# Random-feature attention and a gated MLP in one program: the high part of the gated product is cast by VectorE instead of ScalarE, and the transpose of z moves into a step's MLP share

## The chip, the cores and the metric

The program runs on one core of one Trainium2 chip. Its time is the device time of one execution in microseconds; three executions of the kernel before took 1170.35, 1173.78 and 1174.83 us, median 1173.78 us. The engines are named as in the profile: PE (TensorE matmuls; PEld its weight loads), DVE (VectorE), ACT (ScalarE), POOL (GpSimd), SP (SyncE, which here only issues transfers). Each engine works through its own queue in order and waits on semaphores of the others.

## The reference, cut to what matters

```python
batch, n_heads, seq, head_dim = (8, 8, 576, 64); n_features = 128
n_tokens, d_model, d_ff = (4608, 512, 1536)

def phi(x):                                   # random features
    proj = np.einsum('bhsd,md->bhsm', x, omega)
    h = proj - np.sum(x * x, axis=-1, keepdims=True) / 2.0
    h = h - np.max(h, axis=-1, keepdims=True)
    return np.exp(h) / np.sqrt(m)
q_p, k_p = (phi(q_s), phi(k_s))
kv = np.einsum('bhsm,bhsd->bhmd', k_p, v)
z = np.sum(k_p, axis=2)
num = np.einsum('bhsm,bhmd->bhsd', q_p, kv)
den = np.einsum('bhsm,bhm->bhs', q_p, z)[..., None] + 1e-06
x = (num / den) as [4608, 512]                # attention output = MLP input
g = x @ w_gate;  silu = g * (1.0 / (1.0 + np.exp(-g)));  val = x @ w_val
out = (silu * val) @ w_out
```

All arrays are float32. The MLP is computed with every float32 factor split into a high part (rounded to the PE's faster `fp32r` form) and a low part (the remainder), three matmuls per product: high times high, high times low, low times high.

## The kernel before

**Two halves.** Until about 570 us the program runs the attention in 76 steps, and beside it the MLP for the first three token tiles of 512 (visits 0 to 11: three tiles times four sets of three slices of 128 of the hidden width). After that the six remaining tiles are taken in pairs, with seven products in place of eight per 2x2 block (lines 989 to 1151). The step loop is at lines 1125 to 1150: a step takes one group of 256 rows of q and one of k through transposes (`pt`, L411), projections (`pp`, L434), row maxima and sums on DVE (L448 to L458), exponentials on ACT (`ph`, L470), the accumulation of k's features with v (`kvacc`, L572), and, for q, transposes of the features (`ptq`, L596, copied to `qt`, L598) and the output product (`xt`, L646 or L653).

**What sets the order.** From step `EARLY` on, the tuple `GROUPED` names a step's parts. Between them stand six entries `SHARE`; at each one `give` draws matmuls from the generator `stream` (the MLP) until the MLP is as far as a precomputed course says. The framework's scheduler then fixes each engine's queue when the program is built, beginning from the order of the code; engines do not reorder at run time.

**z.** For batches 4 to 7 (`b >= BPOOL`) the denominators are made by POOL and DVE from rows of z (`q_den`, L528 to L538), so z, the 65th column of the accumulator, must become a row. When a half batch's accumulation ends, `kv_finalize` copies the accumulator out of PSUM on ACT (`kvr`, L486); PE transposes the four z columns (`zp`, L492) in the one PSUM buffer of `ps_att`, ACT copies them (`zs`, L494), SP writes them to DRAM (L496) and `load_z` reads them back broadcast to all partitions (L508). This happens eight times.

**The gated product.** In `stream`, each of the 12 visits has three slices f. For each, PE makes `v` (12 matmuls, L689), DVE multiplies it out of PSUM with the silu of the gate (`sl`, L785), ACT casts the product to its high part (`hh`, L788), POOL subtracts to get the low part (`hl`, L789). The products wait until the next visit's gates are done, when `down` multiplies them with `w_out` (`o`, L698) and DVE adds the result to `acc` (L728). PE's three PSUM buffers `ps_m` hold `g`, `v` and `o` in turn; they come free when ACT has made `sl` from `g` (L765), DVE has read `v` (L785) and DVE has read `o` (L728).

**The handover.** When the last attention transfer has landed, its memory goes to the second half: `first_x` (L844 to L861) loads and splits the next two tiles, and `seven_steps` (L895 to L915) makes the first sums of weights, mostly on DVE, while PE finishes visits 10 and 11. The weights of the first half are converted by a chain over ACT, DVE and POOL (L277 to L295, until about 490 us) and reloaded from DRAM by SP (`wraw`, L334), split by ACT (L251) and POOL (L252).

Of the kernel before, what the change touches and what calls it, by code (L numbers as in the profile page):

```python
# [23 lines left out]
def kernel(  # L24
# [11 lines left out]
    nc = tc.nc  # L36
# [61 lines left out]
    def ps_att(name, shape):  # L98
        return ps_a.tile(shape, F32, name=name, tag="b")
# [30 lines left out]
    def slots(n, kind):  # L130

        if not 0 <= n < NS:
            return []
        return [(i, b, g, (kgroups if kd == "k" else qgroups)[g]) for i, (kd, b, g) in enumerate(steps[n]) if kd == kind]
# [25 lines left out]
    def mm1_us(w):  # L160
        return 3 * NC * (w / 2.4 + 13) * US
# [321 lines left out]
    def kv_finalize(b, a2):  # L483
        acc = kvacc.pop((b, a2))
        raw = att.tile([P, 4, VW], F32, name=f"kvr{b}_{a2}", tag="kvr", bufs=4)
        nc.scalar.copy(raw, acc)  # L486
        for j in range(2):
            kvst[b, 2 * a2 + j] = raw[:, 2 * j : 2 * j + 2, :]
        if b >= BPOOL:

            zp = ps_att(f"zp{b}_{a2}", [4, P])
            nc.tensor.transpose(zp, raw[:, :, D], ident)  # L492
            zs = att.tile([4, P], F32, name=f"zs{b}_{a2}", tag="zs")
            nc.scalar.copy(zs, zp)  # L494
            zd = dram.tile([4, P], F32, name=f"zd{b}_{a2}", tag="zd", bufs=4)
            nc.sync.dma_start(zd, zs)  # L496
            zds[b, a2] = zd

    zds = {}
    zbc = {}  # L500

    def load_z(n):
# [38 lines left out]
    def q_norm(n):  # L541
        n -= NLAG
        for _, b, g, gr in slots(n, "q"):
            if b < BPOOL:
                continue
            dn = dns.pop((b, g))
            phv = box["q", b, g].rearrange("p c (h m) -> p (c h) m", m=M)
            nc.gpsimd.tensor_tensor(
                phv, phv,
                dn[:, 2].rearrange("p c (h o) -> p (c h) o", o=1).broadcast_to([P, 2 * CH, M]),  # L550
                op=ALU.mult,
            )
# [147 lines left out]
    def avail(j):  # L700
        return sum(TILES[j]) <= cols_done[0]
# [4 lines left out]
    def fetch_x(j):  # L706

        xt[j] = [xres.tile([P, NPAIR, T], F32R, name=f"x{e}{j}", tag=f"x{e}") for e in "hl"]
        for c in range(NC):
            raw = moe.tile([P, T], F32, name=f"xraw{j}_{c}", tag="wraw", bufs=3)  # L710
            nc.sync.dma_start(raw, x_dram[j][:, c, :])
            hi, lo = (t[:, c] for t in xt[j])
            nc.scalar.copy(hi, raw)
            nc.gpsimd.tensor_tensor(lo, raw, hi.bitcast(F32), op=ALU.subtract)

    def down(j, k_, ht, wts, next_set, tt):
        fs = sorted(ht)
        po = ps_moe(f"o{j}_{k_}_{tt}", [P, DM])
        for n, f in enumerate(fs):
            need(f, 2)  # L720
            land((f, 2))
            mm2(po, ht[f], weights[f, 2] if wts is None else wts[f], tt, n == 0, n == len(fs) - 1)
        if k_ == 0:
            acc[j, tt] = accp.tile([P, DM], F32, name=f"acc{j}_{tt}", tag="acc")
            nc.scalar.copy(acc[j, tt], po)
        else:
            a_ = acc[j, tt]
            nc.vector.tensor_tensor(a_, po, a_, op=ALU.add)  # L728
        if k_ == (NPF if j in paired else NSET) - 1:
            a_ = acc.pop((j, tt))  # L730
            for o in range(0, P, RES):
                nc.sync.dma_start(rows_of(TILES[j][0] + tt * P + o), a_[o : o + RES, :])
        if next_set is not None and tt == TILES[j][1] // P - 1:
            for f in next_set:
                load_weights(f, 2)

    def stream():

        todo = []
        for vi, (j, s_, k_) in enumerate(visits):  # L740
            nxt = visits[vi + 1] if vi + 1 < len(visits) else None
            new_set = nxt and nxt[1] != s_
            final = nxt is None
            w = TILES[j][1]
            while not avail(j):
                if todo:
                    down(*todo.pop(0))
                    yield MM2
                else:
                    yield None  # L750
            if j not in xt:
                fetch_x(j)
            xs = [t[:, :, 0:w] for t in xt[j]]
            fs = range(s_ * FA, (s_ + 1) * FA)
            pg, ht = {}, {}
            for f in fs:
                need(f, 0)
                land((f, 0))
                pg[f] = ps_moe(f"g{vi}_{f}", [P, T])[:, 0:w]
                mm1(pg[f], weights[f, 0], xs)  # L760
                yield mm1_us(w)

            for f in fs:
                sl = moe.tile([P, T], F32, name=f"sl{vi}_{f}", tag="sl", bufs=FA)[:, 0:w]
                nc.scalar.activation(sl, pg[f], AF.Silu)  # L765
                pg[f] = sl
            if new_set:
                for f in fs:
                    load_weights(nxt[1] * FA + f - fs[0], 0)
            if final:  # L770
                make_seven((0, 0), 0, fetch((0, 1), 0))
            while todo:
                down(*todo.pop(0))
                yield MM2

            if nxt and nxt[0] not in xt and avail(nxt[0]) and last_visit[nxt[0] - NXB] < vi:
                fetch_x(nxt[0])
            for f in fs:
                need(f, 1)
                land((f, 1))  # L780
                pv = ps_moe(f"v{vi}_{f}", [P, T])[:, 0:w]
                mm1(pv, weights[f, 1], xs)
                yield mm1_us(w)
                h = pg[f]
                nc.vector.tensor_tensor(h, pv, h, op=ALU.mult)  # L785
                hh = moe.tile([P, T], F32R, name=f"hh{vi}_{f}", tag="hh", bufs=FA)[:, 0:w]
                hl = moe.tile([P, T], F32R, name=f"hl{vi}_{f}", tag="hl", bufs=FA)[:, 0:w]
                nc.scalar.copy(hh, h)  # L788
                nc.gpsimd.tensor_tensor(hl, h, hh.bitcast(F32), op=ALU.subtract)  # L789
                ht[f] = hh, hl  # L790
                if new_set:
                    load_weights(nxt[1] * FA + f - fs[0], 1)
            if final:
                make_seven((0, 0), 1, fetch((0, 1), 1))
            for f in fs if vi else ():
                land((f, 2))
            wts = {f: weights[f, 2] for f in fs} if vi else None
            then = range(nxt[1] * FA, nxt[1] * FA + FA) if new_set else None
            todo = [(j, k_, ht, wts, then, tt) for tt in range(w // P)]
        yield from pair_rounds(todo)  # L800
# [266 lines left out]
    def give(us):  # L1067
# [40 lines left out]
        SHARE,  # L1108
        SHARE,
        SHARE,  # L1110
        lambda n: q_norm(n + 1),
        q_mult,
        SHARE,
# [72 lines left out]
```

## Time and profile before

| | |
|---|---|
| three executions | 1170.35, 1173.78, 1174.83 us (median 1173.78) |
| the profiled execution | 1174.65 us, of which 1172.6 us from its first to its last instruction |
| granted TensorE clock, mean | 0.998 |
| busy shares of the span | PE 98%, DVE 60%, ACT 58%, POOL 50% |
| steps with MLP work beside them | about 120 to 570 us |
| pairs of tiles | about 620 us to the end |

A row of a group view reads: source line, engine, operation, output and inputs by name, shapes, count; then busy time in us and the mean of one in ns; then the idle time of that engine just before these instructions and what ended it. A row of the timeline reads: start in us, duration in us, engine, line, operation; in brackets how long the engine had been idle and who released it. PE's matmuls overlap, so their durations are not their spacing: a 128x512 matmul is listed with 0.39 us and follows its predecessor after about 0.23 us.

### The profile page before, as it was taken

Reading aid. Unit: us, or ns where it says so; the run is one execution under the profiler, and the core shown is the slowest. Engines: PE = TensorE matmul, PEld = TensorE weight load, DVE = VectorE, ACT = ScalarE, POOL = GpSimd, SP = SyncE. Lnnn points to the kernel's source line nnn. Section 1 sums busy time; section 2 is a strip of 40 time slices with the busy share of each in tenths; the row PEclk is TensorE's granted clock in tenths of the full one; section 3 lists DMA queues with packets and bytes.
Section 4 is the critical chain, followed back from the end, with each engine's and each line's share of the span. In section 5 each row is a group of like instructions: output and inputs, shape, how many; then the busy total and the mean of one; then the engine's idle time right before and its main releaser. Section 6 shows DMA issues by size and latency. Waiting matters only on the chain.

```text
span 1172.6 us, 18833 instructions
## 1 busy us (share of the span) xinstructions
PE 1145.0 (98%) x6633; PEld 948.3 (81%) x6633; DVE 703.3 (60%) x1266; ACT 684.7 (58%) x1541; POOL 588.6 (50%) x515
## 2 busy tenths in 40 slices
PE   8999999999999999999999999999999999999998
PEld 7888778888787778767778788888878888888886
DVE  3777576454666665556373566666566666456654
ACT  4888887877766866857434544444444445444441
POOL 3332353253656775586335655544455543555551
PEclk9999999999999999999999999999999999999999
DMA  6655355654445543431445111124211111211103
GB/s 141 160 135 132 102 161 142 185 151 122 129 130 139 143 140 102 109 86 55 135 109 151 57 55 55 54 65 124 63 50 46 52 52 46 81 55 54 46 18 72
DMA packets 173965, 114.30 MB, mean 97 GB/s; under 512 B 125840, under 2 KB 144304, under 8 KB 173872
## 3 DMA queue, kind: packets, MB, share of 16 engines
q1 hardware_dynamic: 172528, 112.78, 35.1%
q8 instruction: 52, 0.85, 0.3%
q10 hardware_dynamic: 1344, 0.33, 0.1%
q14 instruction: 41, 0.34, 0.1%
HBM read 87.88 MB, written 25.18 MB: 96 GB/s over the span
## 4 chain that ended last, share of the span: by engine, by line
PE 80%; DVE 7%; ACT 4%; POOL 3%; DMA 3%; issue 2%; SPq 0%; POOLq 0%; DVEq 0%; ACTq 0%
PE o L698 22%; PE a L928 16%; PE c L928 8%; PE g L689 6%; PE pp L434 6%; PE kvacc L572 5%; PE v L689 4%; PE d L928 4%; PE pt L411 3%; PE po L613 3%; PE ptq L596 2%; ACT ph L470 2%; PE xt L653 1%; POOL wlo L252 1%; PE xt L646 1%
## 5 line engine op out<-in xcount | busy, mean ns | idle before, releaser
L470 ACT ACTIVATE ph<-pp,st 128x128 f32<-128x128 f32 x576 | 157.3, 387 | 12.8 <-DVE st L458 12.3
L728 DVE TENSOR_TENSOR acc<-o,acc 128x512 f32<-128x512 f32 x156 | 105.8, 685 | 94.6 <-PE o L698 94.2
L418 POOL TENSOR_TENSOR sq<-nat 128x512 f32<-128x512 f32 x72 | 78.1, 1084 | 156.2 <-DVE st L448 113.5
L915 POOL TENSOR_TENSOR wlo<-wspare,whi 128x512 fp32r<-128x512 f32 (+1 forms) x60 | 60.9, 1036 | 117.4 <-ACT whi L914 111.0
L455 DVE TENSOR_REDUCE st<-pp 128x4 f32<-128x512 f32 x144 | 92.8, 683 | 43.2 <-PE pp L434 42.8
L434 PE MATMUL pp<-omT,x 64*128 64x128 f32 x1152 | 96.0, 296 | 3.4 <-ACT x L419 2.3
L252 POOL TENSOR_TENSOR wlo<-wraw,whi 128x512 fp32r<-128x512 f32 x59 | 82.5, 1404 | 26.9 <-ACT whi L251 23.0
L434 PEld LDWEIGHTS pp<-omT,x 64*128 64x128 f32 x1152 | 78.2, 195 | 20.8 <-issue 10.1
L915 POOL TENSOR_TENSOR wlo<-s,whi 128x512 fp32r<-128x512 f32 x64 | 82.4, 1306 | 3.8 <-ACT whi L914 3.8
L1024 ACT COPY late<-a 128x512 f32<-128x512 f32 x72 | 42.2, 586 | 60.0 <-PE a L928 58.8
L698 PE MATMUL o<-whi,late 128*128 128x512 f32 x192 | 74.5, 389 | 0.0
L572 PE MATMUL kvacc<-v,ph 128*128 128x65 f32 x512 | 69.1, 276 | 0.0
L536 DVE TENSOR_REDUCE dj<-jk 128x4 f32<-128x512 f32 x36 | 24.6, 684 | 73.3 <-POOL jk L532 60.7
L572 PEld LDWEIGHTS kvacc<-v,ph 128*128 128x128 f32 x512 | 66.4, 200 | 0.5
L789 POOL TENSOR_TENSOR hl<-sl,hh 128x512 fp32r<-128x512 f32 x36 | 46.9, 1306 | 34.6 <-ACT hh L788 34.6
L291 POOL TENSOR_TENSOR wc<-st 128x512 int32<-128x512 int32 x36 | 37.4, 1040 | 47.7 <-ACT st L289 25.2
L419 ACT COPY x<-pt 128x512 f32<-128x512 f32 x72 | 43.2, 600 | 28.3 <-PE pt L411 26.9
L689 PE MATMUL g<-xh,whi 128*128 128x512 f32 x144 | 59.5, 414 | 0.0
L1028 DVE TENSOR_TENSOR late<-c,late 128x512 f32<-128x512 f32 x25 | 17.3, 692 | 69.7 <-PE c L928 60.6
L698 PE MATMUL o<-whi,hh 128*128 128x512 f32 x144 | 58.4, 406 | 0.5 <-ACT sl L765 0.4
L689 PE MATMUL v<-xh,whi 128*128 128x512 f32 x144 | 57.7, 401 | 0.0
L689 PE MATMUL g<-xh,wlo 128*128 128x512 f32 x144 | 57.4, 398 | 0.0
(255 smaller groups left out, 3355.7 us busy)
## 6 DMA issues: line engine op xcount, KB each, us to landing
wraw<-wscr SPq DMA_DIRECT2D x63, 256.0 KB, 2.7
wspare<-wscr SPq DMA_DIRECT2D x60, 256.0 KB, 2.7
wscr<-wc SPq DMA_DIRECT2D x36, 256.0 KB, 2.2
out_dram<-acc SPq DMA_DIRECT2D x72, 128.0 KB, 2.4
nat<-in_k_dram SPq DMA_DIRECT2D x64, 128.0 KB, 3.0
nat<-in_q_dram SPq DMA_DIRECT2D x64, 128.0 KB, 3.1
v<-in_v_dram SPq DMA_DIRECT2D x62, 128.0 KB, 3.6
st<-in_moe_w_gate_dram SPq DMA_DIRECT2D x12, 512.0 KB, 3.9
```

The source lines that it names most:

```text
L252: nc.gpsimd.tensor_tensor(lo, raw, hi.bitcast(F32), op=ALU.subtract)
L418: nc.gpsimd.tensor_tensor(sq, nat, nat, op=ALU.mult)
L434: nc.tensor.matmul(pp[hh][:, i, c, :], x[r, i, c * P : (c + 1) * P], omT[r], start=True, stop=True)
L455: nc.vector.tensor_reduce(st[:, 1, :, :, hh], pp[hh], axis=AX.X, op=ALU.max, negate=True)
L470: step_end["s"] = nc.scalar.activation(ph[:, c, hh * M : (hh + 1) * M], pp[hh][:, i, c, :], AF.Exp, bias=st[:, 3, i, c, hh : hh + 1], scal ...
L572: nc.tensor.matmul(acc[:, 2 * (pr % 2) + hh, :], ph[:, c, hh * M : (hh + 1) * M], vt[:, 2 * c + j if gr is None else c, hh, :], start=firs ...
L689: nc.tensor.matmul(ps, a_[:, ws], b_[:, c, :], start=n == 0, stop=n == 3 * NC - 1)
L698: nc.tensor.matmul(ps, a_[:, ts_], b_, start=first and n == 0, stop=last and n == 2)
L728: nc.vector.tensor_tensor(a_, po, a_, op=ALU.add)
L789: nc.gpsimd.tensor_tensor(hl, h, hh.bitcast(F32), op=ALU.subtract)
L915: nc.gpsimd.tensor_tensor(lo, src_, hi.bitcast(F32), op=ALU.subtract)
L928: nc.tensor.matmul(ps, a_[:, w_], b_[:, c, :], start=start and c == 0 and m == 0, stop=c == CH - 1 and m == 2, skip_group_check=True,)
```

## The change

1. The cast of the gated product to `hh` (36 instructions, 128x512 each) is issued on VectorE instead of ScalarE. In the code it stands directly behind the multiplication, as before. The casts of the second half (L1011) are left as they are.
2. `kv_finalize` only notes which accumulators were copied. The transposes of z, the copy and the write to DRAM are issued by a new function `z_rows`, which a step calls behind its third `SHARE`; each of the eight is thus issued some MLP matmuls later than before.

```diff
@@ kv_finalize
         if b >= BPOOL:
-
+            zraw[b, a2] = raw
+
+    zraw = {}
+    zds = {}
+
+    def z_rows():
+
+        for (b, a2), raw in zraw.items():
             zp = ps_att(f"zp{b}_{a2}", [4, P])
             nc.tensor.transpose(zp, raw[:, :, D], ident)
             zs = att.tile([4, P], F32, name=f"zs{b}_{a2}", tag="zs")
...
             nc.sync.dma_start(zd, zs)
             zds[b, a2] = zd
-
-    zds = {}
+        zraw.clear()
+
@@ stream
                 nc.vector.tensor_tensor(h, pv, h, op=ALU.mult)
...
-                nc.scalar.copy(hh, h)
+                nc.vector.tensor_copy(hh, h)
                 nc.gpsimd.tensor_tensor(hl, h, hh.bitcast(F32), op=ALU.subtract)
@@ GROUPED
         SHARE,
         SHARE,
         SHARE,
+        lambda n: z_rows(),
         lambda n: q_norm(n + 1),
         q_mult,
         SHARE,
```

The order of the engines' queues moves as follows at the three places of which the prediction speaks. In the changed file the lines behind `kv_finalize` have numbers larger by 7 (the transpose is L499, the cast L795).

PE, the second half of batch 6's k, around 432 us of the trace of before: `pt` are the transposes for the next step, `g` a gate's matmuls, `xt` the output product of a later part of the step.

```order
L411 MATMUL pt_5477<-ident,nat_5190 128x128 x4
L492 MATMUL zp_1_5450<-ident,kvr_1_5448 4x128
L689 MATMUL g_6_5494<-xh_1213,whi_0_4634 128x512
L689 MATMUL g_6_5494<-xl_1214,whi_0_4634 128x512
L689 MATMUL g_6_5494<-xh_1213,wlo_0_4635 128x512
```

```order
L411 MATMUL pt_5471<-ident,nat_5190 128x128 x4
L696 MATMUL g_6_5488<-xh_1213,whi_0_4634 128x512
...
L696 MATMUL g_6_5488<-xh_1213,wlo_0_4635 128x512
L499 MATMUL zp_1_5502<-ident,kvr_1_5448 4x128
L660 MATMUL xt_5_5513<-qt_5_5442,kvr_0_4037 64x256 x2
L434 MATMUL pp_59_5519<-omT,x_5476 128x128
```

Before (first) the transpose of z stood ahead of the gate's twelve matmuls and in the change (second) it stands behind them.

ACT at the step around 521 us, before: `xo` and `qt` are the copies that release the PSUM buffers of the next transposes.

```order
L788 CAST hh_7_6443<-sl_7_6196 128x512
L668 COPY xo_5_7_6474<-xt_5_6471 128x256
L788 CAST hh_8_6544<-sl_8_6198 128x512
L598 COPY qt_6_6492<-ptq_6_6487 128x512
L598 COPY qt_7_6499<-ptq_7_6494 128x512
```

Both casts are gone from this piece of ACT's queue in the change. DVE at the same step, in the change; `st` are the row statistics that ACT's exponentials wait for:

```order
L543 TENSOR_REDUCE dj_0_6527<-jk_0_6525 128x4
L795 CAST hh_7_6443<-sl_7_6196 128x512
L545 RECIPROCAL dj_8_6521<-dj_8_6521 128x4
L544 TENSOR_SCALAR dj_0_6527<-dj_0_6527 128x4
L545 RECIPROCAL dj_0_6527<-dj_0_6527 128x4
L792 TENSOR_TENSOR sl_8_6198<-v_8_6449,sl_8_6198 128x512
L795 CAST hh_8_6544<-sl_8_6198 128x512
L455 TENSOR_REDUCE st_6410<-pp_68_6477 128x4
```

Both casts now stand in DVE's queue ahead of the statistics; before, the other rows stood there in the same order without them.

DVE at the handover, around 588 to 608 us: before, and in the change.

```order
L861 TENSOR_TENSOR t4lo<-first_b_7141,t4hi 128x512
L785 TENSOR_TENSOR sl_10_7084<-v_10_7201,sl_10_7084 128x512
L861 TENSOR_TENSOR b21lo<-first_b_7243,b21hi 128x512
L858 TENSOR_TENSOR first_t_7249<-first_b_7247,first_t_7245 128x512
L861 TENSOR_TENSOR b22lo<-first_b_7247,b22hi 128x512
```

```order
L868 TENSOR_TENSOR t4lo<-first_b_7141,t4hi 128x512
L795 CAST hh_9_7197<-sl_9_7082 128x512
L792 TENSOR_TENSOR sl_10_7084<-v_10_7201,sl_10_7084 128x512
L868 TENSOR_TENSOR b21lo<-first_b_7243,b21hi 128x512
L795 CAST hh_10_7221<-sl_10_7084 128x512
L865 TENSOR_TENSOR first_t_7249<-first_b_7247,first_t_7245 128x512
L868 TENSOR_TENSOR b22lo<-first_b_7247,b22hi 128x512
```

Two casts have entered this piece of DVE's queue, and a third follows behind the next `sl`.

## The prediction

> **What bounds the kernel now.** I read the page's shares first, then busy time by stretches, the waits by engine, and last the timeline around each wait of PE.
>
> ```profile
> PE 1145.0 (98%) x6633; PEld 948.3 (81%) x6633; DVE 703.3 (60%) x1266; ACT 684.7 (58%) x1541; POOL 588.6 (50%) x515
> 510.00:540.00 30.00, 26.82 (x179) 19.94 (x177) 19.70 (x37) 21.17 (x53) 24.43 (x23) 0.94 0.15 42
> 540.00:570.00 30.00, 27.51 (x154) 20.49 (x154) 12.54 (x26) 15.22 (x41) 19.48 (x19) 1.00 0.28 79
> 690.00:720.00 30.00, 30.00 (x134) 24.86 (x133) 18.48 (x27) 13.02 (x24) 16.98 (x14) 1.00 0.18 53
> ```
>
> The columns after the stretch are its length, then busy time of PE, PEld, DVE, ACT and POOL, the granted clock, DMA share and GB/s. From 690 us PE has no hole; nothing there is edited. A change can gain only where PE is idle, and beside the attention that is a few microseconds, in short holes.
>
> ```profile
> L785 DVE TENSOR_TENSOR sl<-v,sl 128x512 f32<-128x512 f32 x36 | 24.7, 686 | 26.2 <-PE v L689 26.2
> L788 ACT CAST hh<-sl 128x512 fp32r<-128x512 f32 x36 | 22.6, 627 | 21.4 <-DVE sl L785 21.2
> PEld zp L492 <- ACT kvr L486: 3.8, 6, 1.4
> PE zp L492 <- ACT kvr L486: 2.1, 3, 1.1
> ```
>
> ACT stands 21.4 us waiting for DVE's product at the cast, and whatever is queued behind it waits too. PE waits for z's copy three times (2.1 us), its weight loads six times (3.8 us).
>
> **Part 1, z.** Eight transposes move behind MLP matmuls, so the copy `kvr` has time. Their copies, DRAM writes and readbacks move with them; SP's `zd` passes loads of q and k, but z is read some steps later, and I cost this at nothing (if that cover were gone, POOL's `jk` would wait). What is gained depends on who is late next.
>
> ```profile
> 394.32 0.27 PE L492 MATMUL zp<-ident,kvr 128*4 128x128 f32 x1 [0.58 <-ACT kvr L486]
> 432.74 0.27 PE L492 MATMUL zp<-ident,kvr 128*4 128x128 f32 x1 [1.14 <-ACT kvr L486]
> 434.06 2.17 ACT L470 ACTIVATE ph<-pp,st 128x128 f32<-128x128 f32 x8 [0.76 <-DVE st L458]
> 436.28 0.94 PE L434 MATMUL pp<-omT,x 64*128 64x128 f32 x12
> 510.75 0.48 PE L689 MATMUL v<-xh,whi 128*128 128x512 f32 x1
> 511.07 0.39 PE L689 MATMUL v<-xl,whi 128*128 128x512 f32 x1
> 511.30 0.40 PE L689 MATMUL v<-xh,wlo 128*128 128x512 f32 x1
> ```
>
> At 394 all 0.58 us should stay. At 432 the projections start at 436.28, just as the exponentials end (434.06 + 2.17 = 436.23), and these wait for DVE: of 1.14 us I keep 0.3. The third hole, at 510 us, leads into part 2's 521 us and counts there. For the three in which only PEld waited I take 0.4, a choice between 0 and 3.8 - 2.1 = 1.7. A lone float32 transpose amid MLP matmuls costs something: behind one, the next spacing is 0.32 us (510.75 to 511.07) and then 0.23 (to 511.30), so 8 x 0.09 = 0.7 at most. Sum: -0.58 - 0.3 - 0.4 + 0.7 = **-0.6 us**; bounds -3.8 (all of PEld's waits, no price) and +0.7.
>
> **Part 2, ACT without the cast.** Four holes of PE stand near casts.
>
> ```profile
> 246.45 0.88 DVE L280 TENSOR_SCALAR wc<-wc 128x512 f32<-128x512 f32 x1 [1.85 <-ACT wc L277]
> 247.80 0.41 PE L646 MATMUL xt<-ident,xn 128*128 128x128 f32 x2 [1.07 <-DVE xn L623]
> L455 DVE TENSOR_REDUCE st<-pp 128x4 f32<-128x512 f32 x144 | 92.8, 683 | 43.2 <-PE pp L434 42.8
> 159.05 0.63 PE L411 MATMUL pt<-ident,nat 128*128 128x128 f32 x4 [2.35 <-issue]
> 518.91 1.25 DVE L537 TENSOR_SCALAR dj<-dj 128x4 f32<-128x4 f32 x1
> 521.00 0.62 ACT L788 CAST hh<-sl 128x512 fp32r<-128x512 f32 x1 [1.95 <-DVE sl L785]
> 522.64 0.66 PE L411 MATMUL pt<-ident,nat 128*128 128x128 f32 x4 [1.89 <-ACT qt L598]
> 523.68 2.17 ACT L470 ACTIVATE ph<-pp,st 128x128 f32<-128x128 f32 x8 [1.09 <-DVE st L458]
> 525.69 0.64 ACT L419 COPY x<-pt 128x512 f32<-128x512 f32 x1
> 527.65 0.60 PE L434 MATMUL pp<-omT,x 64*128 64x128 f32 x6
> 558.75 0.66 PE L596 MATMUL ptq<-ident,ph 128*128 128x128 f32 x4 [2.12 <-ACT xo L668]
> 560.45 0.32 SPq L334 DMA_DIRECT2D wraw<-wscr  x1
> 565.71 0.37 ACT L668 COPY xo<-xt 128x256 f32<-128x256 f32 x1 [2.56 <-DMA xs<-xo]
> L283 DVE TENSOR_SCALAR wc<-wc x36: 415/424/1403, 36.3 to 489.2; 128x512 int32<-128x512 int32 x36
> ```
>
> *247 us:* `xn` stands behind a conversion (L280) that waits 1.85 us for ACT. In the new queue `xn` stands ahead of it: -1.07.
>
> *159 us:* PE waits for the split of `xt` (L675), queued behind a conversion (L286) and one reduction (L455, 0.68 us); in the new queue it precedes the reduction, but not L286. I take -0.7 of the 2.35.
>
> *521 us:* ACT's two casts hold back `qt`, and PE idles 1.89 us. With the casts on DVE that hole closes. But the step's next projections need `x`, copied behind `ph`, and `ph` waits for DVE's statistics. `x` ended at 525.69 + 0.64 = 526.33 and `pp` began at 527.65: 1.32 us of room is all PE can win. Two casts now stand in front of the statistics.
>
> The price of a cast: no DVE copy of this size is in the trace. The nearest row is L283, one operand from SBUF to SBUF with the same 512 elements: 0.42 us as a rule, 1.40 at worst. I take 0.42 per cast where POOL rests and up to 1.40 where it works. Two casts add 0.84 to 2.8 us, so of 1.32 there remain 0.48 to -1.5; I take -0.3 us.
>
> *557 us:* PE waits 2.12 us because `xo` stands behind a cast on ACT. Once that is gone PE runs on, until the copy at 565.71. That copy waits for a transfer whose issue stood behind a weight fetch at 560.45, which waits for POOL. POOL's work is not shortened, so PE stands the 2.12 us there: 0.
>
> The Trainium skill, "SBUF — State Buffer", "Who interferes with whom", says that VectorE's casts from SBUF to SBUF and GpSimd's instructions take one shared port pair by turns, each for its whole length. L283's median and maximum, 0.42 and 1.40, fit a wait of up to one POOL instruction; by the rule every cast issued while POOL works pays this, and would also hold POOL back; the sum would then go toward the slower rival's +6.3, below.
>
> Sum of part 2: -1.07 - 0.7 - 0.3 + 0 = **-2.1 us**; bounds -1.07 - 2.35 - 1.89 - 2.12 = -7.4, and +1.5.
>
> **Part 3, DVE with the cast.** Thirty-six casts give DVE at least 36 x 0.42 = 15.1 us more. Mostly it has room, since its products wait 26.2 us for PE. But where a cast stands directly ahead of the step's reductions, the statistics come later, and in some steps PE waits for them already:
>
> ```profile
> 386.78 1.21 DVE L458 SCALAR_TENSOR_TENSOR st<-st 128x8 f32<-128x8 f32 x1
> 388.03 2.17 ACT L470 ACTIVATE ph<-pp,st 128x128 f32<-128x128 f32 x8 [1.23 <-DVE st L458]
> 389.73 1.67 PE L434 MATMUL pp<-omT,x 64*128 64x128 f32 x16 [0.74 <-ACT ph L470]
> ```
>
> Here a cast adds 0.42. In return POOL's subtraction starts under the reductions, and L458, which took 1.21 us beside POOL, may take less. Two or three such steps: I take **+0.5 us**, between -0.7 and +3 (two casts at 1.40).
>
> **Part 4, the handover.** From 588 to 608 us DVE works almost without a break, and PE twice waits for buffers behind it.
>
> ```profile
> 590.33 0.69 DVE L785 TENSOR_TENSOR sl<-v,sl 128x512 f32<-128x512 f32 x1 [0.37 <-PE v L689]
> 591.62 0.69 DVE L861 TENSOR_TENSOR b21lo<-first_b,b21hi 128x512 fp32r<-128x512 f32 x1 [0.61 <-ACT b21hi L860]
> 592.56 1.47 DVE L858 TENSOR_TENSOR first_t<-first_b,first_t 128x512 f32<-128x512 f32 x1 [0.25 <-DMA first_b<-xs]
> 603.50 0.50 PE L698 MATMUL o<-whi,hh 128*128 128x512 f32 x1 [0.36 <-ACT sl L765]
> 607.28 1.88 DVE L728 TENSOR_TENSOR acc<-o,acc 128x512 f32<-128x512 f32 x3
> ```
>
> Three casts enter this piece. DVE's own idle there is 0.37 + 0.61 + 0.25 = 1.23 us, so at 0.42 each they may vanish; at 1.40 each they cost 4.2. The start of the chain, the last attention transfer, moves with PE and gives nothing back. I take 3 x 0.42 = **+1.3 us**, since the third cast falls behind the idle time and the first two only partly into it.
>
> **Sum.** -0.6 - 2.1 + 0.5 + 1.3 = -0.9 us, against the profiled 1174.65 us (span 1172.6 and 2.05 around it): 1173.8. The profiled execution lies 0.87 us above the median of the three, so the forecast for the median is **1172.9 us**.
>
> **Rivals.** *PE keeps what ACT gives back.* If the later waits move forward as well, part 1 gives 2.1 and part 2 its 7.4, less 1.3 at the handover: -8.2, **1165.6 us**. For it: these are real holes of PE, and every later stage is fed by PE. Against it: the rows at 525.69 and 565.71, where the next wait stands within 8 us.
>
> ```profile
> 519.00:523.00 4.00, 1.91 (x11) 1.42 (x12) 3.93 (x6) 1.64 (x4) 4.00 (x4) 1.00 0.10 35
> 524.00:525.00 1.00, 1.00 (x4) 0.74 (x3) 0.18 (x1) 1.00 (x6) 0.74 (x1) 0.50 0.00 0
> 555.00:559.00 4.00, 1.88 (x14) 1.13 (x11) 2.08 (x4) 1.32 (x4) 3.92 (x4) 1.00 0.24 56
> ```
>
> In the same case the clock may stay up: after the hole at 521 us the granted clock fell to 0.50, and 0.94 over 30 us (510 to 540) says that 1.8 us of clock were lost; after an equal hole at 557 it stayed 1.00. Without the first loss, 1163.8. The Trainium skill, "TensorE: Matmul & The Clock Gate", "What's actually happening", states a window of about 3.4 us that runs freely; that one of two equal holes was punished agrees with it.
>
> *VectorE becomes the bound (slower).* If casts mostly meet POOL at work, then part 4 costs 4.2, part 3 its 3 and the step at 521 its 1.5: +8.7, less 0.6 of z and 1.8 of the first two holes: +6.3, **1180.1 us**. It decides from a mean cast of about 1.1 us. For it: POOL is busy 24.4 of 30 us from 510 to 540. Against it: POOL's next instruction is often the subtraction that waits for this very cast.
>
> *Nothing moves.* The products are not needed before the next visit, so the cast's place is hidden, and z's wait returns one part later: **1173.8 us**.
>
> **How the numbers follow.** Forecast 0.50, PE keeps it 0.25, VectorE bounds 0.14, nothing moves 0.11. Half a per cent, 5.9 us, is about what a measurement of this kernel can tell from no change. Faster than that: 0.22 of the first rival and 0.03 of the forecast's edge, 0.25; slower: 0.12 and 0.02, 0.14; the rest 0.61. The likeliest case alone spans 1168 to 1177; the range, 1165.2 to 1179.5, takes in half the first rival and stops short of the second's end.
>
> **What would show it.** Right: casts on DVE near 0.42 us median and 1.4 at most; no wait of PE for `kvr`; the hole at 247 gone; `pp` after 521 us waiting for `x` or `ph`; more waiting for `xo` near 566; PE's holes at 600 to 610 longer by about 1 us. Wrong: PE's idle time from 510 to 570 smaller by over 3 us, or casts with a mean above 1 us.

## The result and the profile after

Seven executions of the change took 1176.77 to 1183.97 us, median 1179.99; seven of the kernel before, on the same chip, 1170.35 to 1174.83, median 1173.78. The ratio is 1.0055 (95% interval 1.0038 to 1.0072): slower by 0.55%, some 6.5 us. The forecast was 1172.9 us with a range to 1179.5, so the change went the other way and ended half a microsecond outside the range. The profiled execution of the change is the slowest of its seven (1183.97 us, span 1182.2). Behind `kv_finalize` its lines are seven higher: the cast is L795, the product L792, the subtraction L796.

Shares of the span, and two stretches (columns as before):

```profile
PE 1149.0 (97%) x6633; PEld 951.2 (80%) x6633; DVE 721.2 (61%) x1302; ACT 665.6 (56%) x1505; POOL 590.6 (50%) x515
510.00:540.00 30.00, 25.30 (x155) 19.09 (x154) 19.19 (x40) 13.90 (x40) 24.26 (x23) 0.89 0.26 75
540.00:570.00 30.00, 29.59 (x189) 23.02 (x189) 16.97 (x36) 21.14 (x54) 20.54 (x19) 1.00 0.18 52
```

ACT lost 19 us of work and DVE gained 18, as planned. PE's idle time from 510 to 570 us, 5.67 us before, is 5.11. Who PE waited for, in the change and then in the kernel before (sum, times, longest):

```profile
PE pp L434 <- ACT ph L470: 4.7, 4, 1.9
PE xt L660 <- ACT x L419: 4.7, 1, 4.7
PE o L705 <- ACT sl L772: 1.6, 1, 1.6
PE ptq L603 <- POOL hl L796: 0.9, 1, 0.9
```

```profile
PE pp L434 <- ACT ph L470: 1.0, 2, 0.7
PE o L698 <- ACT sl L765: 0.4, 1, 0.4
```

The waits for z's copy and for `qt` are gone; waits for the exponentials and for the `x` behind them have taken their place. Both hang on DVE's row statistics. The groups between 120 and 600 us, first before, then after:

```profile
L458 DVE SCALAR_TENSOR_TENSOR st<-st 128x8 f32<-128x8 f32 x47 | 14.8, 314 | 1.6
L457 DVE SCALAR_TENSOR_TENSOR st<-st 128x8 f32<-128x8 f32 x47 | 12.7, 271 | 1.5
L470 ACT ACTIVATE ph<-pp,st 128x128 f32<-128x128 f32 x379 | 103.2, 384 | 10.1 <-DVE st L458 9.8
```

```profile
L457 DVE SCALAR_TENSOR_TENSOR st<-st 128x8 f32<-128x8 f32 x47 | 13.3, 283 | 1.6
L458 DVE SCALAR_TENSOR_TENSOR st<-st 128x8 f32<-128x8 f32 x47 | 12.8, 272 | 1.6
L470 ACT ACTIVATE ph<-pp,st 128x128 f32<-128x128 f32 x376 | 102.4, 386 | 24.3 <-DVE st L458 24.0
```

ACT stood 10.1 us in front of the exponentials before and 24.3 us after. Part of that is time in which ACT used to cast, and is no loss by itself: experiment 10 below has 16.2 us there and is faster than before. Nor did L457 and L458 grow over the 47 steps (27.5 us together before, 26.1 after); what counts is when they end in single steps. The costliest place is the step that I had followed through 521 us. First before, then in the change, where it lies 7 us later:

```profile
520.29 0.68 DVE L785 TENSOR_TENSOR sl<-v,sl 128x512 f32<-128x512 f32 x1
522.09 1.27 POOL L789 TENSOR_TENSOR hl<-sl,hh 128x512 fp32r<-128x512 f32 x1
522.20 1.18 DVE L457 SCALAR_TENSOR_TENSOR st<-st 128x8 f32<-128x8 f32 x1
523.42 0.17 DVE L458 SCALAR_TENSOR_TENSOR st<-st 128x8 f32<-128x8 f32 x1
```

```profile
526.49 0.68 DVE L792 TENSOR_TENSOR sl<-v,sl 128x512 f32<-128x512 f32 x1
527.20 0.73 DVE L795 CAST hh<-sl 128x512 fp32r<-128x512 f32 x1
527.85 1.27 DVE L455 TENSOR_REDUCE st<-pp 128x4 f32<-128x512 f32 x2
529.16 0.69 DVE L457 SCALAR_TENSOR_TENSOR st<-st 128x8 f32<-128x8 f32 x1
529.79 1.25 POOL L796 TENSOR_TENSOR hl<-sl,hh 128x512 fp32r<-128x512 f32 x1
529.88 1.19 DVE L458 SCALAR_TENSOR_TENSOR st<-st 128x8 f32<-128x8 f32 x1
531.16 2.17 ACT L470 ACTIVATE ph<-pp,st 128x128 f32<-128x128 f32 x8 [5.14 <-DVE st L458]
533.17 0.64 ACT L419 COPY x<-pt 128x512 f32<-128x512 f32 x1
533.86 1.97 PE L660 MATMUL xt<-qt,kvr 128*64 128x256 f32 x6 [4.70 <-ACT x L419]
535.77 2.08 PE L434 MATMUL pp<-omT,x 64*128 64x128 f32 x16
```

From the product to the end of L458 4.58 us pass, against 3.30 before. Of the difference the cast is 0.65 us and L457 and L458 together are 0.53 (1.88 against 1.35): GpSimd's subtraction ran beside them before too. PE's gate matmuls, which before filled the time up to `x`, have run earlier, so its idle time has come together in one hole of 4.70 us. And from the end of that hole on the clock is halved, just under the projections:

```profile
528.00:532.00 4.00, 1.17 (x5) 0.35 (x3) 3.60 (x5) 0.84 (x4) 3.30 (x4) 1.00 0.00 0
532.00:536.00 4.00, 2.14 (x8) 0.99 (x10) 1.89 (x4) 3.97 (x10) 3.59 (x4) 0.59 0.00 0
536.00:540.00 4.00, 4.00 (x26) 3.59 (x27) 2.90 (x8) 1.10 (x4) 2.90 (x3) 0.55 0.26 78
```

To see where time went I compare the end of each step's `x` copy (L419) with the same step before, from the step at 132 us on. The profiled executions had by then drifted apart by up to 3.5 us, at loads before 45 us that no edit touches; that is taken off. Worked out from the timelines, us against before; the last column is PE's first matmul of the pairs:

| kernel | 252 | 307 | 342 | 379 | 405 | 440 | 484 | 511 | 544 | 652 |
|---|---|---|---|---|---|---|---|---|---|---|
| the change | +0.5 | +2.6 | +2.7 | +1.3 | +7.0 | +7.9 | +8.5 | +8.7 | +11.5 | +11.4 |
| cast alone | -0.2 | +1.4 | +1.4 | -0.4 | +1.9 | +2.8 | +2.8 | +2.7 | +5.7 | +5.3 |
| z alone | -0.6 | -0.1 | -0.1 | +2.2 | +2.4 | +2.5 | +3.1 | +3.1 | +3.1 | +2.7 |
| casts behind the statistics | -0.2 | +0.3 | +0.3 | -1.3 | -1.3 | -2.1 | -2.2 | -2.3 | -4.2 | -4.6 |

The lower three rows are experiments 1, 2 and 6. Of the 6.1 us by which the change falls behind the cast alone, 3.3 come between 379 and 405 us. There its profile has 6.8 us at half clock, behind a wait of 1.95 us for exponentials, and the profile of the cast alone has none. That profile is also the execution with the lowest clock of its seven (0.991; the others 0.994 to 0.997), so the table overstates what the change loses there as a rule.

### The profile page after: what moved, and what is told of

Read it like the earlier page. It is cut to its first block, busy times and chain, and to the rows that moved or that the text cites. A ratio compares the mean times of both kernels' runs of the same rounds, so it can differ in the third digit from the quotient of the medians.

```text
span 1182.2 us, 18867 instructions
## 1 busy us (share of the span) xinstructions
PE 1149.0 (97%) x6633; PEld 951.2 (80%) x6633; DVE 721.2 (61%) x1302; ACT 665.6 (56%) x1505; POOL 590.6 (50%) x515
## 4 chain that ended last, share of the span: by engine, by line
PE 78%; DVE 8%; ACT 5%; POOL 3%; issue 2%; DMA 2%; SPq 0%; POOLq 0%; ACTq 0%; DVEq 0%
PE o L705 22%; PE a L935 15%; PE c L935 8%; PE pp L434 6%; PE v L696 5%; PE g L696 4%; PE kvacc L579 4%; PE d L935 4%; PE ptq L603 3%; PE pt L411 2%; PE po L620 2%; ACT ph L470 2%; PE xt L660 1%; DVE st L455 1%; DMA nat<-in_k_dram 1%
## 5 line engine op out<-in xcount | busy, mean ns | idle before, releaser
L434 PEld LDWEIGHTS pp<-omT,x 64*128 64x128 f32 x1152 | 79.5, 195 | 26.5 <-issue 10.1
L796 POOL TENSOR_TENSOR hl<-sl,hh 128x512 fp32r<-128x512 f32 x36 | 47.7, 1326 | 44.3 <-DVE hh L795 33.0
L605 ACT COPY qt<-ptq 128x512 f32<-128x512 f32 x72 | 41.9, 590 | 33.3 <-PE ptq L603 33.0
L419 ACT COPY x<-pt 128x512 f32<-128x512 f32 x72 | 43.5, 604 | 27.5 <-PE pt L411 26.3
```

Of the source, the lines that this page charges most:

```text
L434: nc.tensor.matmul(pp[hh][:, i, c, :], x[r, i, c * P : (c + 1) * P], omT[r], start=True, stop=True)
```

## Experiments

Times are medians; the us behind a ratio are (ratio - 1) x 1173. The ratio on record is not the quotient of the two medians: in experiment 1 the medians differ by 4.7 us, which is what the expectations use, and the ratio gives 3.4. Each execution's mean granted clock is on record as well. What I call the clock's part is (1 - clock) x span, averaged over the executions, less the same of the kernel before in that comparison; "by the means" is the difference of the two average times. The clock's part is rough: the clocks are rounded to 0.001, which is 1.2 us, a difference is uncertain by some 1.5 to 2 us, and a half-clock stretch that lies partly in a hole of PE costs less than it counts. My theory after the result (A): the casts make the row statistics, and with them exponentials and projections, late in the tight steps. Rivals: B, the moved z costs it; C, half-clock stretches are the loss.

### 1 to 4: the parts

Experiment 1, the cast alone:

```diff
-                nc.scalar.copy(hh, h)
+                nc.vector.tensor_copy(hh, h)
```

> The cast on VectorE alone; z stays as before. Theory A (the casts make the row statistics, and with them the exponentials and projections, late in the tight steps): most of the change's +6.2 us is here, 1178 to 1181 us, and PE's waits for ACT's exponentials ahead of the projections stay near 4.7 us. Rival B (the moved transposes of z cost it): at most 1175 us. Rival C (the loss is mainly half-clock stretches behind holes of PE): 1176 to 1181 us, and the time differs from before by what the granted clock differs, (1 - clock) x span, within 2 us.

1177.75 us, ratio 1.0029 (1.0010 to 1.0049), +3.4. The time lies between what A and B had said. By the means it is 4.5 us, of which 2.3 are the clock's part; the 2.2 that remain are just over the 2 us that C allowed, so C explains about half of this.

Experiment 2, z alone: the change's first half, with `nc.scalar.copy(hh, h)`.

> The transposes of z moved alone; the cast stays on ScalarE. Theory A: 1172 to 1174 us, the three waits of PE for z's copy gone (2.1 us) and given back in part by the next wait. Rival B: 1177 us or more. Rival C says nothing of its own here: the same as the kernel before, 1173 to 1174 us.

1175.77 us, ratio 1.0025 (1.0010 to 1.0040), +2.9. The parts add up: 3.4 + 2.9 = 6.3 of 6.5. So the cast is about half of it and z the other half, though this time too lies between what A and B had said. For z's half C falls as the cause: this kernel's profile has one half-clock stretch, as before's has, and is still 2.7 us behind, and the clock's part is -1.3 us.

Experiment 3, z moved and no cast:

```diff
-                nc.vector.tensor_tensor(h, pv, h, op=ALU.mult)
+                nc.vector.tensor_tensor(hh, pv, h, op=ALU.mult)
...
-                nc.vector.tensor_copy(hh, h)
```

> z moved, and no cast at all: VectorE's product is written straight into the high part's buffer, and GpSimd subtracts it from the silu, so the low part is not the remainder (left out: the 36 casts). ScalarE is relieved as in the change, and VectorE is not loaded. Theory A: faster than before, 1168 to 1172 us, since what ScalarE's relief gives (the holes at 247 and 557 us) stays and no statistics come later. Rival B: 1177 or more, as z is moved here too. Rival C: 1174 to 1180 us, since the holes that the relief opens at the next wait drop the clock here as well. A fourth reading, that ScalarE's relief gives nothing because the next wait stands right behind: 1173 us.

1174.56 us, ratio 1.0007 (0.9990 to 1.0024), +0.8. Against z alone, taking the cast off ACT without giving it to anyone is worth 2.1 us (the intervals overlap); giving it to DVE costs 5.7 against that. A had said 1168 to 1172, but z was moved here too.

Experiment 4, the change with 15 casts back on ScalarE:

```diff
-                nc.vector.tensor_copy(hh, h)
+                (nc.scalar.copy if vi in (5, 6, 7, 8, 10) else nc.vector.tensor_copy)(hh, h)
```

> The change, but in visits 5, 6, 7, 8 and 10 the cast is back on ScalarE (15 of 36). Theory A: these are the visits whose casts stand ahead of statistics that PE waits for (holes at 391, 441, 529 us) and of the handover (611 us), so the loss goes: 1171 to 1174 us. If each cast costs alike on VectorE wherever it stands: 21/36 of the loss stays, 1177 us. Rival B: 1178 us or more. Rival C: 1173 to 1177 us, by how the clock falls.

1175.86 us, ratio 1.0020 (1.0002 to 1.0037), +2.3: what z alone costs, and above A's 1171 to 1174, which had no price for z. The loss on the cast's side stands in visits 5 to 8 and 10.

### 5, 7, 8: where z and the cast cost

In the profile of z alone 2.3 us are lost around 373 us. SP and ACT there, with PE's hole, first z alone, then the kernel before:

```profile
366.43 1.60 SPq L233 DMA_DIRECT2D st<-in_moe_w_val_dram  x1
368.93 0.32 SPq L334 DMA_DIRECT2D wraw<-wscr  x1
370.27 0.62 ACT L470 ACTIVATE ph<-pp,st 128x128 f32<-128x128 f32 x2 [2.34 <-DVE st L458]
372.70 0.62 ACT L251 CAST whi<-wraw 128x512 fp32r<-128x512 f32 x1 [1.80 <-DMA wraw<-wscr]
373.22 1.65 ACT L470 ACTIVATE ph<-pp,st 128x128 f32<-128x128 f32 x6
374.41 1.67 PE L434 MATMUL pp<-omT,x 64*128 64x128 f32 x16 [1.78 <-ACT ph L470]
```

```profile
367.19 0.33 SPq L334 DMA_DIRECT2D wraw<-wscr  x1
368.52 0.39 SPq L233 DMA_DIRECT2D st<-in_moe_w_val_dram  x1
370.33 0.62 ACT L251 CAST whi<-wraw 128x512 fp32r<-128x512 f32 x1 [3.59 <-DMA wraw<-wscr]
371.34 2.17 ACT L470 ACTIVATE ph<-pp,st 128x128 f32<-128x128 f32 x8
373.05 1.67 PE L434 MATMUL pp<-omT,x 64*128 64x128 f32 x16 [0.27 <-ACT ph L470]
```

With z's transfers elsewhere in SP's queue, the scheduler put the 512 KB weight load ahead of the weight read `wraw`, and on ACT put the cast that waits for `wraw` between the second and the third exponential. Experiment 5 turns that one z at once:

```diff
             zraw[b, a2] = raw
+            if (b, a2) == (5, 1):
+                z_rows()
```

> The transposes of z moved, the cast on ScalarE, but one of the eight z (batch 5, second half) is turned at once, as before. In the profile of z alone moved, the loss lies at one place: PE waits 1.78 us for the exponentials at 373 us (0.28 before), where ScalarE's queue has a weight cast amid the exponentials, and that cast waits for a weight read that SP now issues behind a 512 KB weight load. This kernel has the order of before on both queues there. Theory Z (the order of the transfers on SP and with it ScalarE's costs what z costs): the hole at 373 us is back near 0.3 us, and the time 1172.5 to 1174 us. Rival (the lone transposes cost it, or z's later readback): seven of eight stay, so 1175.5 us or more.

In its profile both orders and the hole are as before:

```profile
370.68 0.62 ACT L251 CAST whi<-wraw 128x512 fp32r<-128x512 f32 x1 [3.70 <-DMA wraw<-wscr]
373.40 1.67 PE L434 MATMUL pp<-omT,x 64*128 64x128 f32 x16 [0.39 <-ACT ph L470]
```

But the time is 1175.68 us, ratio 1.0023 (1.0008 to 1.0038), +2.7. So the queue order explains the 2.3 us of that profile and not all that z costs over many executions. Its profile has 0.6 us at 484 us, where PE waits for a `qt` behind z's copy, and two half-clock stretches from 132 us on where before's has one. The clock's part is +1.3 us here, against -1.3 with all of z moved. Without it, by the means, z costs 1.2 us here and 4.2 there: the mended order may have brought what the profile says, and a lower clock taken it back. Why the clock was lower stays open.

Experiment 7, z as before, the cast on VectorE in visits 5 to 8 alone:

```diff
-                nc.scalar.copy(hh, h)
+                (nc.vector.tensor_copy if vi in (5, 6, 7, 8) else nc.scalar.copy)(hh, h)
```

> z as before, casts on VectorE in visits 5 to 8 only (12 of 36). Theory A: most of what the cast costs stands here: by the shift of the steps between 340 and 545 us, +4 us: 1176 to 1178 us. If each cast costs alike: a third of 4.7, 1174.6 us.

1176.53 us, ratio 1.0034 (1.0019 to 1.0049), +4.0. Twelve casts cost what 36 do. By the means it is 3.6 us, and the clock's part is 3.6 as well (95% interval 2.0 to 5.4). The profile has a hole of 4.64 us and with it 6.8 us at half clock, the first 1.7 of them still in the hole; before, a hole of 1.89 us and 3.4 us at half clock. So in these visits C is not a rival to A but most or all of its price: the late statistics make one long hole, and the clock falls behind it.

Experiment 8, experiment 5 with casts on VectorE in visits 0, 1 and 9:

```diff
-                nc.scalar.copy(hh, h)
+                (nc.vector.tensor_copy if vi in (0, 1, 9) else nc.scalar.copy)(hh, h)
```

> A version meant to beat both: z moved except that one, casts on VectorE only in visits 0, 1 and 9, where the profiles show that ScalarE's relief closes holes (157 us: 2.34 to 0.5, then 0.7 us given back at 169 us; 557 us: 2.1, of which 1.1 to 1.2 us stayed) and where no statistics that PE waits for come later. Theory A with Z: 1170.5 to 1172.5 us. If VectorE's casts cost alike everywhere: 1174 us or more.

1172.49 us, ratio 0.9990 (0.9974 to 1.0006). 3.9 us better than experiment 5, but not told from before: no version to keep.

### 6, 9, 10, 11: the place or the engine

Experiment 6 leaves z as before and orders each cast of visits 0 to 8 behind the next L458:

```diff
                 nc.vector.tensor_tensor(h, pv, h, op=ALU.mult)
-                hh = ...; hl = ...
-                nc.scalar.copy(hh, h)
-                nc.gpsimd.tensor_tensor(hl, h, hh.bitcast(F32), op=ALU.subtract)
+                later.append((vi, f, w, h, ht))
+                if vi > 8:
+                    split()
...
+    def split(after=None):
+        with tc.issue_after(after.ins) if after else ExitStack():
+            while later:
+                vi, f, w, h, ht = later.pop(0)
+                hh = ...; hl = ...
+                nc.vector.tensor_copy(hh, h)
+                nc.gpsimd.tensor_tensor(hl, h, hh.bitcast(F32), op=ALU.subtract)
+                ht[f] = hh, hl
... GROUPED
         st_max,
+        lambda n: split(biased[0]),
         st_exp,
```

`split` is also called ahead of `down`, for casts that are still left.

> z as before, all casts on VectorE, but in visits 0 to 8 each is ordered behind the next row statistics (L458) instead of directly behind its product; GpSimd's subtraction is later with it. Theory A (the casts stand ahead of the statistics and make the exponentials late): the waits for exponentials of the run with the cast alone (1.28 us at 391 us) and the long hole at 525 us (4.6 us) shrink to those of before; 1172 to 1175 us. Rival P (what costs is VectorE's time and the ports it shares with GpSimd, wherever the cast stands): 1177 to 1178.5 us as with the cast directly behind. Rival D (the low parts come too late for the products that use them): PE waits for hl, over 1179 us.

1166.69 us, ratio 0.9958 (0.9944 to 0.9972), -4.9: faster than before, which none of the three readings had said, and 8.3 us from experiment 1, with the same casts on the same engine. The clock's part is -1.6 us. The same step as above:

```profile
512.66 0.67 DVE L800 TENSOR_TENSOR sl<-v,sl 128x512 f32<-128x512 f32 x1
513.25 1.28 DVE L455 TENSOR_REDUCE st<-pp 128x4 f32<-128x512 f32 x2
514.57 0.17 DVE L457 SCALAR_TENSOR_TENSOR st<-st 128x8 f32<-128x8 f32 x1
514.77 0.17 DVE L458 SCALAR_TENSOR_TENSOR st<-st 128x8 f32<-128x8 f32 x1
514.85 0.76 DVE L745 CAST hh<-sl 128x512 fp32r<-128x512 f32 x2
515.42 2.57 POOL L746 TENSOR_TENSOR hl<-sl,hh 128x512 fp32r<-128x512 f32 x2 [0.82 <-DVE hh L745]
517.74 1.08 PE L653 MATMUL xt<-qt,kvr 128*64 128x256 f32 x6 [0.51 <-ACT x L419]
```

From the product to the end of L458 it is 2.28 us, against 4.58. Of the 2.30 between them the cast itself is 0.65 (527.20 to 527.85); 1.54 stand in L457 and L458, 0.69 and 1.19 against 0.17 each. L458 ran beside GpSimd's subtraction, which the cast had released. Over the steps:

```profile
L458 DVE SCALAR_TENSOR_TENSOR st<-st 128x8 f32<-128x8 f32 x47 | 10.5, 223 | 1.6
L457 DVE SCALAR_TENSOR_TENSOR st<-st 128x8 f32<-128x8 f32 x47 | 10.5, 223 | 1.6
L470 ACT ACTIVATE ph<-pp,st 128x128 f32<-128x128 f32 x376 | 102.6, 384 | 12.5 <-DVE st L458 12.3
```

Experiment 9 keeps the cast on ScalarE, ordered behind the exponentials; against experiment 6:

```diff
-                nc.vector.tensor_copy(hh, h)
+                nc.scalar.copy(hh, h)
...
-        lambda n: split(biased[0]),
         st_exp,
+        lambda n: split(step_end["s"]),
```

> z as before, the cast stays on ScalarE, but in visits 0 to 8 it is ordered behind the step's exponentials; GpSimd's subtraction comes later with it. This separates the place from the engine in the run with the casts behind the statistics (1166.7 us). Reading Q (the place alone gives the gain: the subtraction no longer stands beside the statistics, and ScalarE no longer waits at the cast): 1166 to 1169 us. Reading R (ScalarE's relief gives it, and it needs VectorE): 1171 to 1174 us.

1171.84 us where before took 1175.03: ratio 0.9981 (0.9962 to 1.0000), -2.2. The median lies in R's range, but before was 2.2 us slower in this comparison than in that of experiment 6, so by the ratio it is neither reading: the place gives at most a part. The clock's part is -2.9 us, so nothing is left beside it. The statistics are as slow as before there (27.3 us for both rows), since the subtraction now falls beside other ones:

```profile
L457 DVE SCALAR_TENSOR_TENSOR st<-st 128x8 f32<-128x8 f32 x47 | 14.2, 302 | 1.6
L458 DVE SCALAR_TENSOR_TENSOR st<-st 128x8 f32<-128x8 f32 x47 | 13.1, 279 | 1.6
```

Experiment 10, the change with the casts behind the statistics; against experiment 6 only z differs:

```diff
         SHARE,
+        lambda n: z_rows(),
         lambda n: q_norm(n + 1),
```

> The change with one thing altered: in visits 0 to 8 the cast on VectorE is ordered behind the row statistics. z is moved as in the change. If z costs the same whatever the casts do (2.9 us): 1169 to 1170 us. If z's cost comes only through statistics that are late anyway: 1166 to 1167.5 us. If the place of the cast was not the cause of the change's loss: 1176 us or more.

1172.12 us beside 1175.03, ratio 0.9972 (0.9954 to 0.9991), -3.3; the median lies in none of the three ranges. The change's loss is gone, with z moved and the same casts on the same engine. So the place was the cause of the cast's part of the loss; z still takes 1.6 us of what experiment 6 gained (the intervals overlap).

Experiment 11, no cast, z as before:

```diff
-                nc.vector.tensor_tensor(h, pv, h, op=ALU.mult)
+                nc.vector.tensor_tensor(hh, pv, h, op=ALU.mult)
...
-                nc.scalar.copy(hh, h)
```

> z as before and no cast at all (left out: the 36 casts; the high part is the product, the low part is not the remainder); GpSimd subtracts directly behind the product. Reading V (VectorE's casts delay the statistics by their own time): without them the time falls below that of the casts behind the statistics, 1164 to 1167 us. Reading G (GpSimd's subtraction beside the statistics delays them as well, so a kernel without any cast still has late statistics): 1170 to 1173 us.

1172.86 us beside 1175.03, ratio 0.9987 (0.9966 to 1.0008), -1.5, as reading G has it. With no cast on any engine the kernel is slower than with casts in the right place (the intervals overlap slightly with experiment 6, not with experiment 12). The cast's own time cannot be all.

### 12: a version that beats both

From experiment 6, visit 1 directly and visits 10 and 11 on ScalarE:

```diff
-                nc.vector.tensor_copy(hh, h)
+                (nc.vector.tensor_copy if vi < 10 else nc.scalar.copy)(hh, h)
...
-                if vi > 8:
+                if vi > 8 or vi == 1:
```

> A version meant to beat the one with the casts behind the statistics (1166.7 us): visit 1's casts directly behind the products again (PE waited 0.7 us for its low parts at 203 us, 1.4 us by the shift of the steps), and the casts of visits 10 and 11 on ScalarE (the holes at 594 and 600 us are 1.2 and 0.6 us there, 0.4 and 0.1 before). Theory A: 1164 to 1166 us. If the handover and visit 1 gain nothing: 1166 to 1167.5 us.

1163.56 us beside 1175.03, ratio 0.9919 (0.9893 to 0.9945), -9.5 us. PE's idle time over the span is 16.5 us, against 22.9 before and 28.5 in the change.

### 13 to 15: the cast's time or the subtraction

Three kernels without the subtractions; `hh` stands for `hl`:

```diff
-                nc.gpsimd.tensor_tensor(hl, h, hh.bitcast(F32), op=ALU.subtract)
-                ht[f] = hh, hl
+                ht[f] = hh, hh
```

> The kernel before without GpSimd's 36 subtractions (left out: the low part; the high part is multiplied in its place). The base for the next two. Reading G (GpSimd's subtraction, started right behind a product, runs beside the row statistics and makes them late): faster than before, 1168 to 1171 us. Reading V (VectorE's cast time in front of the statistics is what costs): as before, 1172 to 1174 us.

> The cast alone on VectorE, directly behind the product, without the subtractions. With them it cost 4.7 us against before. Reading V: again 4 us or more over the run without subtractions and the cast on ScalarE. Reading G: not slower than that run by more than 1 us, or faster by up to 3, since ScalarE's relief is then free.

> The casts on VectorE behind the statistics in visits 0 to 8, without the subtractions. With them the place was worth 11 us (1177.75 to 1166.69). Reading V: the place is worth 7 us or more here too. Reading G: under 3 us, since no subtraction is moved with the cast.

| (against before, us) | with subtraction | without |
|---|---|---|
| cast on ScalarE | 0 | -8.4 (ratio 0.9928, 0.9911 to 0.9944) |
| cast on VectorE, directly behind | +3.4 (1.0029, 1.0010 to 1.0049) | -6.5 (0.9945, 0.9926 to 0.9963) |
| cast on VectorE, behind the statistics | -4.9 (0.9958, 0.9944 to 0.9972) | -9.1 (0.9922, 0.9903 to 0.9942) |

The medians without it are 1164.90, 1167.11 and 1163.26 us; the first is below what either reading had said. The place is worth 8.3 us with the subtraction and 2.6 without: as reading G has it, most of it hangs on GpSimd's subtraction. The difference of 5.7 us is uncertain by about 4. The cast's direct place costs 3.4 with and 2.0 without; these lie between the readings, and each is uncertain by 2 to 3 us, so how this price divides is not settled. That the subtractions, on an engine that is busy for half the span, cost the kernel before 8.4 us is the larger finding. It is not the price of late statistics alone: the clock's part is 3.1 us, and of the 7.2 us by which the profile is ahead at 652 us, 1.8 stand already at 168 us, behind the place where PE had waited 2.35 us for the split of `xt` (0.59 now).

## Why the prediction was wrong

- **Part 1, z: -0.6 forecast, +2.9 measured.** The step that failed is "Their copies, DRAM writes and readbacks move with them ... I cost this at nothing". The waits for `zp` did go. But I read the queues at the transposes only; the scheduler had also exchanged a weight load and a weight read on SP, and moved a waiting cast amid the exponentials; the change has the same order, and PE waits 1.11 us there. My upper bound, +0.7, had no term for a changed order elsewhere. After the order was mended (experiment 5), 2.7 us remained by the ratio, about half of it the clock's part; the cause of the rest is open.
- **Part 2, 247 us: -1.07.** The hole went, but not by the cast: with the cast alone it is 1.41 us, with z alone it is gone. I had read the order of both edits together.
- **Part 2, 159 us: -0.7.** 2.35 us became 0.50, and 0.74 came back at 169 us as a wait for exponentials; with the cast alone the steps were 0.6 us ahead at 168. The size came out right, in part by luck: the hole closed further than I had said, and I had not seen what came back.
- **Part 2, 521 us: -0.3, bounds to +1.5.** With the cast alone the steps lose 3.1 us there (+2.7 to +5.7). "1.32 us of room is all PE can win" took the time of `x` as fixed: in experiment 6 the statistics end 1.0 us sooner behind the product than before (2.28 against 3.30), and the steps gain 1.9 us there. As a loss I counted only the two casts. L457 and L458 lengthened as well, and the hole, 0.46 + 1.89 us before, came together and drew two half-clock spells onto the projections; before, the one spell had fallen on gate matmuls that ran while `x` was still awaited.
- **Part 2, 557 us: 0.** The hole closed. PE did not stop for `xo` near 566 us, as I had said, but 0.93 us for a low part (`hl`) at 574. The change stands at +11.5 us at 544 us and +11.4 at 652 although the handover between added up to 1.7, so some 1 to 2 us were kept: too low.
- **The price of a cast.** Median 0.43 us and at most 1.50, against 0.42 and 1.40 taken:

```profile
L795 DVE CAST hh<-sl x36: 413/426/1500, 140.0 to 628.9; 128x512 fp32r<-128x512 f32 x36
```

- **Part 3: +0.5, bounds -0.7 to +3.** Mis-sized: visits 5 to 8 alone cost 4.0 (2.2 to 5.8), with the step at 521. The step that failed here is that a late statistic was priced by the casts in front of it alone. The clock stands in my working only on the faster side, in the first rival; in these visits it is most or all of the loss. The sentence "L458, which took 1.21 us beside POOL, may take less" came true at the step quoted (0.17 us, while L457 went from 0.34 to 0.92) and, for both rows together, over all steps. At 521 it went the other way, from 0.17 to 1.19: there the cast frees the subtraction just ahead of L458. The Trainium skill, "SBUF — State Buffer", "Who interferes with whom", says beside the rule that I weighed for the cast also that a VectorE instruction with two inputs in SBUF contends with a GpSimd instruction that reads SBUF, and that reductions do not. The rows agree: L457, with two small inputs, takes 0.16 to 1.18 us, and the reduction L448, of 128x512, always the same.

```profile
L457 DVE SCALAR_TENSOR_TENSOR st<-st x47: 156/168/1184, 125.5 to 548.5; 128x8 f32<-128x8 f32 x47
L448 DVE TENSOR_REDUCE st<-sq x46: 672/678/682, 126.7 to 541.0; 128x8 f32<-128x512 f32 x46
```

- **Part 4, the handover: +1.3.** PE's two holes grew from 0.36 and 0.13 to 1.59 and 0.61 us, +1.7, and fell below 0.3 with those casts on ScalarE in experiment 12. Right in place and size.
- **The rivals.** "VectorE becomes the bound", 1180.1 us, gave the time, yet its condition, a mean cast of 1.1 us, was not met (0.61): the right sum by another way, half of it z. "PE keeps what ACT gives back", 1165.6, is near what experiment 6 reached (1166.69) once the casts stood behind the statistics, but partly by another way: the statistics themselves are shorter there. The marks that I gave for "wrong", PE idle 3 us less or casts above 1 us, did not come, and the forecast was wrong all the same: I had set none for late statistics, nor for the clock.

## What to carry to other kernels

When an instruction moves to an in-order engine, ask which short instruction of the critical chain stands behind it, and what it releases on a third engine that then runs beside that chain; here the same casts cost 3.4 us directly behind the product and gained 4.9 behind the statistics. Compare the order on every queue, SP's too, edit by edit and over the whole piece, since a scheduler changes places that the edit does not touch. Closing some of PE's holes can move the rest of its idle time together, and a long hole can cost its clock as well: compare the granted clock of all executions before a loss is put down to a wait alone.

## What the runs showed of the hardware

- VectorE's 8-element `scalar_tensor_tensor` took 0.17 us as a rule and up to 1.2 beside GpSimd, seven times as much, while 512-element reductions did not change. Leaving out 36 subtractions of about 1.3 us on GpSimd, an engine that is busy for half the span, made the kernel 8.4 us faster, by all that they held up and not by this alone.
- The time lost to the granted clock in a profile, (1 - clock) x time, came behind holes of PE in lots of 1.71 us: 1.71 in the kernel before, 1.71, 1.71, 3.41 and 3.41 in the change, 3.41 behind each of the three holes of 4.6 to 4.7 us (the change, experiments 1 and 7), none from 120 to 1150 us in experiments 6, 9, 10 and 12 to 15, which had no hole over 2.2 us. The length of the hole does not settle it: one of 3.1 us lost one lot and one of 3.3 us two (experiments 11 and 3), and holes between 0.6 and 2.4 us lost one or two lots in some executions and none in others. At half clock a lot is 3.4 us long, which agrees with the window of about 3.4 us that the Trainium skill states ("TensorE: Matmul & The Clock Gate", "What's actually happening").
- Up to the step at 117 us all these kernels run the same program, and their profiled executions still differed there by up to 5 us, at waits for the first loads; this limits what a comparison of this kernel can tell.
